# Seven-product FFN1 in two more tiles, seeded PSUM in the last two, and adding DMA stores for four output tiles

## The chip, the cores and the metric

One core of a Trainium2 chip runs the kernel. The metric is the device time of one execution in microseconds (us). Five engines take part, each with its own queue of instructions in a fixed order: PE (matrix multiply), ACT (activations and copies), DVE (elementwise), POOL (here almost only issuing DMAs) and SP (issuing DMAs). PE writes to PSUM, which ACT and DVE read.

## The reference

Attention with 16 extra "beacon" keys in front of each sequence, followed by a two-layer network with an ELU between, on 8 batches, 8 heads, 576 tokens and head size 64:

```python
k_all = np.concatenate([beacon_k, k], axis=2)          # 16 + 576 keys
v_all = np.concatenate([beacon_v, v], axis=2)
scores = scale * np.matmul(q, k_all.transpose(0, 1, 3, 2))
scores = np.where(causal, -1000000000.0, scores)
a = np.exp(scores - scores.max(-1, keepdims=True))
a /= a.sum(-1, keepdims=True) + 1e-09
attn_out = np.matmul(a, v_all)
x = attn_out.transpose(0, 2, 1, 3).reshape(4608, 512)
h = x @ w_in                                           # FFN1: 512 -> 2048
g = np.where(h > 0.0, h, np.exp(np.minimum(h, 0.0)) - 1.0)
out = g @ w_out                                        # FFN2: 2048 -> 512, fp32
```

## The kernel before

All matrix work is in fp16 or bf16 with fp32 sums in PSUM. The whole program is one list of words, written out as a string and passed to `run`; each word calls one step, and every engine executes its instructions in the order in which the list issues them. A word names a step and its arguments: `P.8.2.5` is step `P` for tile 8, group 2, phase 5. A `.v` at the end puts the step on DVE where it would otherwise be on ACT.

The 4608 tokens are cut into ten tiles: tiles 0 and 1 have 256 tokens, tiles 2 to 9 have 512. Batches of attention (steps `T`, `S`, `x`, `m`, `D`, `L`, `n`, `W`, `M`) fill the tiles' activations `xT` and run interleaved with the network of earlier tiles.

FFN1 of a tile has two forms.

- **Plain**: `F.t.i` multiplies 128 rows of `w_in` with all 512 tokens: 4 matmuls of 128x512 into one PSUM bank (`hps`). ACT takes the exponential (`e`), ACT or DVE the ReLU (`u`), and DVE joins them into the ELU (`k`). Sixteen `F` make a tile.
- **Seven products** (Strassen's scheme, in tiles 8 and 9): a group `g` covers the work of four `F` as a 2x2 block product, with 7 phases `P.t.g.0` to `P.t.g.6` of 4 matmuls of 128x256 each. The four quarters of the result are sums of products that share terms. `PF` lists for each phase the accumulator (0 or 1) and the operands. `K` takes the intermediate sums out: after phases 0, 2 and 3 a copy to SBUF on ACT (`fm`, in the buffers named `kst`/`qst` in the trace), after phases 1, 4 and 5 a DVE addition of accumulator 1 or 0 and such a copy (`hb`). `E`, `U` and `V` then do for each quarter what `e`, `u` and `k` do; they read `hb` in SBUF, or, for phase 6, PSUM. `X` (four per tile, DVE) and `H` (16, DVE) prepare the operands' differences.

FFN2 uses seven products in all tiles: `Q.t.k0.k1` issues matmuls k0 to k1 of the tile's 112, each 128x256, into two accumulators (`ops`). `Z` (DVE, four per tile) prepares differences, and `J` takes results out in the same manner as `K`: phases 0, 2, 3 are copied to SBUF (`sm`), phases 1, 4, 5 are added on DVE to such a copy (`osb`, line 635), phase 6 is copied, and `osb` is stored to `out` by SP.

PSUM has eight banks: two for `hps`, two for `ops`, and two double banks with the tag `S` for attention. Both accumulators of a group of seven products hold the two `hps` banks.

Of the kernel before, what the change touches and what calls it, by code (L numbers as in the profile page):

```python
# [17 lines left out]
def kernel(  # L18
# [11 lines left out]
    nc = tc.nc  # L30
# [487 lines left out]
    def flat(y):  # L518
        return y.rearrange("c n w -> c (n w)")
# [101 lines left out]

    @step
    def J(t, ph, eng="s"):

        if ph in (0, 2, 3):
            sm[t, ph] = melt.tile([P, 2, HM], FP32, tag="sm", name="sm")
            for q_, y in both(xy[t, PH[ph][0]]):
                (nc.scalar.copy if eng == "s" else nc.vector.tensor_copy)(out=sm[t, ph][:, q_, :], in_=y)
            return
        osb = melt.tile([P, 2, HM], FP32, tag="osb", name="osb")  # L630
        for q_, y in both(xy[t, PH[ph][0]]):
            if ph == 6:
                (nc.scalar.copy if eng == "s" else nc.vector.tensor_copy)(out=osb[:, q_, :], in_=y)
            else:
                nc.vector.tensor_tensor(  # L635
                    out=osb[:, q_, :], in0=y, in1=sm[t, {1: 0, 4: 3, 5: 2}[ph]][:, q_, :], op=ALU.add)
        i, m_ = {1: (0, 0), 4: (1, 1), 5: (0, 1), 6: (1, 0)}[ph]
        row = (tiles[t][0] if t > 1 else 0) + 256 * i
        nc.sync.dma_start(
            out=out[row:row + 256, HM * m_:HM * (m_ + 1)].rearrange("(q p) m -> p q m", p=P), in_=osb)  # L640
# [45 lines left out]
    def X_(t, n, eng="v"):  # L686
# [6 lines left out]
          (0, (1, 0), 3, False), (1, 4, (1, 1), False), (0, (1, 1), 4, False)]  # L693
    hx, fm, hb = {}, {}, {}

    @step
    def P_(t, g, ph):
        if (t, g, 0) not in hx:
            for n_ in (0, 1) if g % 2 == 0 else (1, 0):
                hx[t, g, n_] = bank("hps", name="hps").rearrange("c (n w) -> c n w", n=2)  # L700
        n_, a_, b_, first = PF[ph]
        for c in range(2):
# [9 lines left out]
    def K_(t, g, ph, eng="s"):  # L712
        src = flat(hx[t, g, PF[ph][0]])
# [8 lines left out]
    def hsrc(t, g, ph):  # L722
        return flat(hx[t, g, 0]) if ph == 6 else hb[t, g, ph]
# [76 lines left out]
    wm.4 wm.4 warm.4 wm.4 lq.0.0.0.4 lq.0.1.0.4 wm.4 warm.4 ident lq.0.0.4.8 wm.4 T.0.1.0 bt  # L800
    warm.4 lq.0.1.4.8 bk cb.0.3 T.0.0.0 cb.0.1 cb.0.0 ck.0.1.0 S.0.1.0 ck.0.0.0 T.0.1.1 x.0.1.0
    S.0.0.0 x.0.0.0 T.0.0.1 cq.0.1.1 S.0.1.2 cq.0.0.1 T.0.3.0 S.0.0.2 x.0.1.2 T.0.2.0 x.0.0.2
    cq.0.3.0 S.0.0.3 cb.0.2 lq.1.0.0.4 S.0.3.0 T.0.3.1 cq.0.2.0 x.0.0.3 lv.0.0.1 cq.0.3.1
    x.0.3.0 T.0.2.1 S.0.0.1 tri wm.4 x.0.0.1 S.0.3.2 x.0.3.2 S.0.1.3 cq.0.2.1 x.0.1.3 wm.4 wm.4
    S.0.2.0 wm.4 wm.4 x.0.2.0 S.0.3.3 wm.4 x.0.3.3 S.0.2.3 x.0.2.3 wm.4 m.0.3.0 S.0.3.1 cb.1.0
    x.0.3.1 lv.0.2 m.0.1.0 m.0.2.0 m.0.0.0 L.0.A m.0.1.2 n.0.A m.0.0.2 T.1.0.0 wi.2 m.0.3.2
    cq.1.0.0 S.0.2.1 W.0.A.1 x.0.2.1 W.0.A.0 S.0.1.1 x.0.1.1 T.1.1.0 M.0.A.1 S.0.2.2 M.0.A.0
    x.0.2.2 F.0.5 cq.1.1.0 e.0.5 lv.0.3.4 m.0.2.2 wi.1 m.0.0.3 m.0.1.3 S.1.5 S.1.1 x.1.5 m.0.3.3
    F.0.4 x.1.1 lq.1.0.4.8 wi.0 m.0.2.3 L.0.B cb.1.1 e.0.4 W.0.B.1 n.0.B S.1.3 cb.1.3 u.0.4.v
    M.0.B.1 u.0.5.v F.0.2 x.1.3 e.0.2 r.0.2 S.1.4 x.1.4 S.1.0 x.1.0 F.0.3 T.1.3.0 ck.1.3.0  # L810
    W.0.B.0 g.0.2 wi.3 k.0.4 S.1.12 m.1.0.0 k.0.5 M.0.B.0 e.0.3 F.0.1 x.1.12 T.1.2.0 S.1.10
# [133 lines left out]
```

## Time and profile before

| what | value |
|---|---|
| time, median of 3 runs | 330.33 us (329.78 to 330.42) |
| the profiled execution | 329.86 us, with a span of 328.2 us |
| instructions | 8827 |
| granted TensorE clock | 1.00 throughout |
| data moved by DMA | 34.65 MB, mean 106 GB/s |
| DMA engines' busy share | 0.9 or more in the first 18 of 40 slices, 0.0 to 0.3 in the last 16 |

The span is what the profile covers; 1.66 us of the execution lie around it. "Busy" counts overlapping instructions of an engine once. Two instructions that follow each other without a wait overlap by some tens of nanoseconds, so that the step from start to start is shorter than the mean duration that a row gives.

### The profile page before, as it was taken

Reading aid. Unit: us, or ns where it says so; the run is one execution under the profiler, and the core shown is the slowest. Engines: PE = TensorE matmul, PEld = TensorE weight load, DVE = VectorE, ACT = ScalarE, POOL = GpSimd, SP = SyncE. Lnnn points to the kernel's source line nnn. Section 1 sums busy time; section 2 is a strip of 40 time slices with the busy share of each in tenths; the row PEclk is TensorE's granted clock in tenths of the full one; section 3 lists DMA queues with packets and bytes.
Section 4 is the critical chain, followed back from the end, with each engine's and each line's share of the span. In section 5 each row is a group of like instructions: output and inputs, shape, how many; then the busy total and the mean of one; then the engine's idle time right before and its main releaser. Section 6 shows DMA issues by size and latency. Waiting matters only on the chain.

```text
span 328.2 us, 8827 instructions
## 1 busy us (share of the span) xinstructions
PE 318.5 (97%) x3648; PEld 215.7 (66%) x3648; DVE 296.9 (90%) x527; ACT 276.4 (84%) x449; POOL 85.2 (26%) x109
## 2 busy tenths in 40 slices
PE   7879999999999999999999999999999999999995
PEld 4656766566555655566555665566665888888884
DVE  2677998999998999999989989999999999999992
ACT  2979999998889897999999888988699598889930
POOL 8973791742705626004010500000000000000000
PEclk9999999999999999999999999999999999999999
DMA  9999999999999999995922792010110021111113
GB/s 115 169 190 206 172 167 185 151 151 154 174 173 154 136 172 151 188 116 61 160 82 58 77 106 84 12 34 2 66 34 33 2 96 34 34 65 34 35 64 128
DMA packets 130520, 34.65 MB, mean 106 GB/s; under 512 B 112816, under 2 KB 130480, under 8 KB 130480
## 3 DMA queue, kind: packets, MB, share of 16 engines
q0 software_dynamic: 95840, 18.49, 69.1%
q1 hardware_dynamic: 33920, 15.34, 23.8%
q8 instruction: 28, 0.46, 0.6%
q10 hardware_dynamic: 720, 0.26, 0.3%
q14 instruction: 12, 0.10, 0.1%
HBM read 37.22 MB, written 15.34 MB: 160 GB/s over the span
## 4 chain that ended last, share of the span: by engine, by line
PE 72%; DMA 12%; ACT 7%; POOL 4%; DVE 3%; issue 2%; DVEq 0%; POOLq 0%
PE ops L618 27%; PE hps L514 22%; DMA v<-in_v_dram 10%; PE hps L706 8%; PE sc L318 5%; ACT et L333 5%; PE ut L376 5%; PE sx L618 2%; POOL scr L769 1%; POOL v L149 1%; DMA kst<-in_k_dram 1%; ACT e L524 1%; POOL w_out L163 1%; DVE qkp L396 1%; PE lt L422 1%
## 5 line engine op out<-in xcount | busy, mean ns | idle before, releaser
L333 ACT ACTIVATE et<-sc 128x1024 f16<-128x1024 f32 (+2 forms) x114 | 104.2, 968 | 8.1 <-PE sc L318 7.6
L514 PE MATMUL hps<-xT,w_in 128*128 128x512 f16 (+1 forms) x512 | 110.7, 353 | 0.3 <-DVE gt L556 0.3
L618 PEld LDWEIGHTS <-gt 128*128 128x128 f16 x864 | 83.0, 98 | 21.1 <-issue 2.9
L524 ACT ACTIVATE e<-hps 128x512 f32<-128x512 f32 x112 | 66.7, 615 | 9.0 <-PE hps L514 4.1
L514 PEld LDWEIGHTS <-w_in 128*128 128x128 f16 x512 | 46.8, 98 | 39.0 <-issue 5.5
L544 DVE SCALAR_TENSOR_TENSOR gt<-e,r 128x512 f16<-128x512 f32 x103 | 68.6, 683 | 2.2 <-ACT e L524 0.7
L618 PE MATMUL ops<-w_out,gt 128*128 128x256 f16 x416 | 54.7, 273 | 0.0
L618 PE MATMUL ops<-wt,gt 128*128 128x256 f16 x400 | 53.6, 273 | 0.0
L530 ACT ACTIVATE r<-hps 128x512 f16<-128x512 f32 x74 | 45.0, 616 | 4.5 <-PE hps L514 4.3
L149 POOL DMA_DIRECT2D v<-in_v_dram x40 | 36.4, 1016 | 3.5 <-DMA v<-in_v_dram 1.9
L566 DVE TENSOR_TENSOR gt<-gt 128x2048 f16<-128x2048 f16 (+1 forms) x30 | 33.1, 1110 | 0.1
L338 DVE TENSOR_TENSOR et<-et,triu 128x1024 f16<-128x1024 f16 (+4 forms) x66 | 26.6, 447 | 1.8 <-ACT et L333 1.7
L532 DVE TENSOR_SCALAR r<-hps 128x512 f16<-128x512 f32 x29 | 19.9, 685 | 4.0 <-ACT e L524 3.2
L376 PEld LDWEIGHTS <-v 128*32 128x32 f16 (+1 forms) x800 | 17.2, 96 | 9.4 <-issue 1.2
L745 DVE SCALAR_TENSOR_TENSOR gt<-e,r 128x512 f16<-128x512 f32 x32 | 21.5, 683 | 0.5 <-ACT kst L716 0.4
L376 PE MATMUL ut<-et,v 128*32 128x464 f16 (+3 forms) x560 | 21.1, 296 | 0.3 <-DMA v<-in_v_dram 0.3
L396 DVE TENSOR_TENSOR qkp<-qkp,et 128x1344 f16<-128x1344 f16 (+2 forms) x33 | 19.2, 583 | 0.4
L635 DVE TENSOR_TENSOR osb<-ops,sm 128x512 f32<-128x512 f32 x26 | 17.7, 682 | 1.3 <-PE ops L618 1.3
L716 ACT COPY kst<-hps 128x512 f32<-128x512 f32 x24 | 13.9, 589 | 4.8 <-PE hps L706 4.6
L474 DVE TENSOR_TENSOR xT<-ut,rl 128x672 f16<-128x672 f32 (+12 forms) x26 | 16.4, 669 | 0.7 <-PE ut L376 0.4
L618 PE MATMUL ops<-w_out,s 128*128 128x256 f16 x128 | 16.9, 273 | 0.0
L618 PEld LDWEIGHTS <-s 128*128 128x128 f16 x144 | 13.9, 98 | 2.5
(118 smaller groups left out, 415.7 us busy)
## 6 DMA issues: line engine op xcount, KB each, us to landing
out_dram<-osb SPq DMA_DIRECT2D x35, 256.0 KB, 2.2
v<-in_v_dram POOLq DMA_DIRECT2D x24, 128.0 KB, 11.8
scr<-in_q_dram POOLq DMA_DIRECT2D x5, 576.0 KB, 16.2
scr<-in_k_dram POOLq DMA_DIRECT2D x5, 576.0 KB, 18.1
w_in<-in_moe_w_in_dram POOLq DMA_DIRECT2D x8, 256.0 KB, 8.7
w_out<-in_moe_w_out_dram POOLq DMA_DIRECT2D x4, 512.0 KB, 10.5
qst<-in_q_dram POOLq DMA_DIRECT2D x4, 288.0 KB, 9.6
kst<-in_k_dram POOLq DMA_DIRECT2D x4, 288.0 KB, 10.0
```

The source lines that it names most:

```text
L149: nc.gpsimd.dma_start(out=vt[b][r0:r0 + n, j, :, :], in_=v[b, :, ilo[j]:ilo[j] + n, :].rearrange("h s d -> s h d"),)
L333: nc.scalar.activation(out=ets[b, d][:, :, a - EC2 * d:e - EC2 * d], in_=sc[b, g][:, :, a - c0:e - c0], func=AFT.Exp, bias=0.0, scale=SCALE)
L338: nc.vector.tensor_tensor(out=o, in0=o, in1=i, op=ALU.mult)
L376: nc.tensor.matmul(out=t[32 * i:32 * (i + 1), a - qa:e - qa], lhsT=ones[0:kc[j], :] if half is None else v16[0:kc[j], j, h, half:D:2], rhs ...
L396: nc.vector.tensor_tensor(out=o, in0=t[0:rows, :, a:e] if n == 0 else o, in1=t[0:rows, :, col:col + e - a], op=ALU.add)
L514: nc.tensor.matmul(out=h[:, n_, :], lhsT=w_in16[:, cc, P * fc:P * (fc + 1)], rhs=xt[k][:, cc, a - TT * k:e - TT * k], start=(cc == 0), sto ...
L524: nc.scalar.activation(out=eb[t, i], in_=flat(hp[t, i]), func=AFT.Exp, bias=0.0, scale=1.0)
L530: nc.scalar.activation(out=rb[t, i], in_=flat(hp[t, i]), func=AFT.Relu, bias=0.0, scale=1.0)
L544: nc.vector.scalar_tensor_tensor(out=half(t, i), in0=eb[t, i], scalar=1.0, in1=rb[t, i], op0=ALU.subtract, op1=ALU.min)
L566: (nc.vector if eng == "v" else nc.gpsimd).tensor_tensor(out=o_, in0=a_, in1=b_, op=op_)
L618: nc.tensor.matmul(out=half_of(xy[t, n_], qd), lhsT=lw[:, P * qd:P * (qd + 1)], rhs=wt_[:, c, :], start=(first and c == 0 and (qd == 0 or ...
L706: nc.tensor.matmul(out=hx[t, g, n_][:, c, :], lhsT=lw, rhs=rh, start=(first and c == 0 and k_ == 0), stop=(k_ == 1), skip_group_check=True)
```

## The change

Three edits, and a new order of the list.

1. Seven products for 15 groups instead of 8: the first three groups of tile 6 and all four of tile 7 take this form, besides tiles 8 and 9. In tile 6 the plain form is left for `F.6.12` to `F.6.15`. For each of these groups 16 matmuls of 128x512 become 28 of 128x256.
2. In tiles 8 and 9 phase 0 gets an accumulator of its own (`sa`, in the tag `S`, which attention has left by then). `K.t.g.0` is now a ScalarE copy from `sa` to a `hps` bank, and phase 1 accumulates on it. `K.t.g.1`, the DVE addition, is gone, and `E` and `U` of phase 1 read that bank. Phases 3 and 5 take another `hps` bank.
3. In tiles 5 to 8 the partial sums are no longer added on DVE. The copy `sm` is stored to its block of `out` by SP, the second part is copied by ACT to `osb`, and POOL issues a DMA that adds it to what stands in `out`.

```diff
+    TA = (5,6,7,8)
...
     def J(t, ph, eng="s"):
...
+            if t in TA:
+                nc.sync.dma_start(out=block(t, {0: 1, 3: 4, 2: 5}[ph]), in_=sm[t, ph])
             return
         osb = melt.tile([P, 2, HM], FP32, tag="osb", name="osb")
         for q_, y in both(xy[t, PH[ph][0]]):
-            if ph == 6:
+            if ph == 6 or t in TA:
                 (nc.scalar.copy if eng == "s" else nc.vector.tensor_copy)(out=osb[:, q_, :], in_=y)
...
+        if ph == 6 or t not in TA:
+            nc.sync.dma_start(out=block(t, ph), in_=osb)
+        else:
+            nc.gpsimd.dma_start(out=block(t, ph), in_=osb, accum_op=ALU.add)
...
+    PA = [0, 1, 0, 2, 0, 2, 0]
...
     def P_(t, g, ph):
-        if (t, g, 0) not in hx:
+        seed = t >= 8
+        if seed and ph == 0:
+            hx[t, g, 0] = psum.tile([P, 2, 512], FP32, tag="S", name="sa")[:, 0, :].rearrange("c (n w) -> c n w", n=2)
+        if seed and ph == 3:
+            hx[t, g, 2] = bank("hps", name="hps").rearrange("c (n w) -> c n w", n=2)
+        if not seed and (t, g, 0) not in hx:
...
         n_, a_, b_, first = PF[ph]
+        if seed:
+            n_ = PA[ph]
+            first = first and ph != 1
...
     def K_(t, g, ph, eng="s"):
-        src = flat(hx[t, g, PF[ph][0]])
+        if t >= 8 and ph == 0:
+            hx[t, g, 1] = bank("hps", name="hps").rearrange("c (n w) -> c n w", n=2)
+            nc.scalar.copy(out=flat(hx[t, g, 1]), in_=flat(hx[t, g, 0]))
+            return
+        src = flat(hx[t, g, (PA[ph] if t >= 8 else PF[ph][0])])
...
     def hsrc(t, g, ph):
+        if t >= 8 and ph == 1:
+            return flat(hx[t, g, 1])
...
-    Q.9.49.56 J.9.2.v Z.9.4.1 Z.9.4.0 J.8.5 Q.9.63.70 J.9.3 Q.9.70.77 Q.9.77.84 Q.9.84.91 J.9.4
+    Z.9.1.1 Q.9.0.7 Q.9.7.14 Z.9.2.0 J.8.6 Q.9.14.21 J.8.5 Z.9.2.1 Q.9.21.28 J.9.0 Q.9.28.35
```

The list is new from its first words on: the attention of the first batches, which ReLUs stand on DVE, and the places of the loads differ too. What each engine executes stays the same in kind outside the three edits, apart from four FFN1 results whose ELU was taken by `r` and `g` (both on DVE) and is now taken by `u` and `k`.

ACT, in FFN1 of tile 9, before. `kst0` and `qst0` are SBUF buffers for the sums, `hps` PSUM banks, `e` and `r` the two parts of the ELU:

```order
L716 COPY kst0_88<-hps_5264 128x512
L735 ACTIVATE r_5319<-kst0_88 128x512
L728 ACTIVATE e_5321<-kst0_88 128x512
L728 ACTIVATE e_5335<-qst0_87 128x512
L735 ACTIVATE r_5341<-hps_5263 128x512
L735 ACTIVATE r_5358<-qst0_87 128x512
L728 ACTIVATE e_5360<-hps_5263 128x512
L716 COPY kst0_88<-hps_5353 128x512
```

The same engine in the last group of tile 9 now; `sa` is the accumulator of the phases 0, 2, 4 and 6:

```order
L733 COPY hps_5484<-sa_5458 128x512
L752 ACTIVATE e_5498<-qst0_87 128x512
L738 COPY kst0_88<-hps_5477 128x512
L738 COPY kst0_88<-sa_5458 128x512
L635 COPY sm_5521<-ops_5278 128x512
L759 ACTIVATE r_5525<-hps_5484 128x512
L752 ACTIVATE e_5527<-hps_5484 128x512
L759 ACTIVATE r_5529<-qst0_87 128x512
```

The first copy of a group goes from PSUM to PSUM, and one exponential and one ReLU of the group read PSUM where they read SBUF; ACT's number of instructions for such a group is the same.

DVE at the last group of tile 9 before (`gt` is the ELU's result):

```order
L719 TENSOR_TENSOR kst0_88<-hps_5353,kst0_88 128x512
L745 SCALAR_TENSOR_TENSOR gt_5172<-e_5360,r_5341 128x2x256
L719 TENSOR_TENSOR qst0_87<-hps_5352,kst0_88 128x512
L745 SCALAR_TENSOR_TENSOR gt_5172<-e_5414,r_5399 128x2x256
L745 SCALAR_TENSOR_TENSOR gt_5172<-e_5428,r_5426 128x2x256
L566 TENSOR_TENSOR gt_5172<-gt_5172 128x4x256
```

and now:

```order
L741 TENSOR_TENSOR qst0_87<-hps_5477,kst0_88 128x512
L769 SCALAR_TENSOR_TENSOR gt_5321<-e_5498,r_5482 128x2x256
L741 TENSOR_TENSOR kst0_88<-sa_5458,kst0_88 128x512
L566 TENSOR_TENSOR s3_86<-gt_5321 128x1024
L769 SCALAR_TENSOR_TENSOR gt_5321<-e_5531,r_5529 128x2x256
L769 SCALAR_TENSOR_TENSOR gt_5321<-e_5527,r_5525 128x2x256
```

Of the three additions of a group (line 719, now 741) two are left in tiles 8 and 9.

The end of POOL's queue, now; `v` is the load of a batch's values, which was the last entry before:

```order
L149 DMA v_3635<-in_v_dram 80x8x64
L649 DMA out_dram<-osb 128x2x256 x12
```

The twelve adding stores stand behind all loads, so that no load waits for them.

246 lines of the change are left out of this document (127 added, 119 removed).

## The prediction

> **What bounds the kernel now.** The first view is the busy time of each engine by stages of the span. Its columns are PE, PE's weight loads, DVE, ACT and POOL, then the granted clock, the DMA engines' share and GB/s.
>
> ```profile
> 20.00:40.00 20.00, 17.96 (x332) 12.93 (x325) 16.21 (x35) 18.11 (x25) 10.52 (x16) 1.00 1.40 193
> 40.00:60.00 20.00, 19.85 (x348) 12.77 (x346) 18.14 (x34) 19.39 (x32) 10.93 (x12) 1.00 1.69 172
> 60.00:200.00 140.00, 139.08 (x1466) 84.07 (x1465) 133.49 (x228) 127.09 (x197) 46.10 (x52) 1.00 1.44 131
> 200.00:240.00 40.00, 39.75 (x430) 24.26 (x431) 38.51 (x64) 32.65 (x55) 0.00 (x0) 1.00 0.10 34
> 240.00:300.00 60.00, 60.00 (x543) 48.65 (x544) 59.13 (x102) 51.09 (x98) 0.00 (x0) 1.00 0.13 42
> 300.00:312.00 12.00, 12.00 (x111) 10.64 (x109) 11.65 (x20) 11.71 (x23) 0.00 (x0) 1.00 0.12 38
> ```
>
> PE is never idle from 240 to 312 us and for 1.2 us in the 180 us before. DVE is close behind: 0.9 us idle of 60 in the stage where tiles 8 and 9 run seven products. A busy PE row is modelled, so the second view is the chain of work that ended last, where pieces stand from start to start.
>
> ```profile
> 250.54 0.76 PE ops L618 x7
> 251.30 1.73 PE hps L514 x8
> 253.03 0.77 PE ops L618 x7
> ...
> 281.41 1.53 PE ops L618 x14
> 282.94 0.87 PE hps L706 x8
> 283.81 0.77 PE ops L618 x7
> ...
> 322.83 1.76 PE sx L618 x16
> ```
>
> Each piece begins where the one before ends: PE is a gapless queue at 1.73/8 = 0.216 us for a 128x512 matmul (plain FFN1) and 0.87/8 = 0.109 us for a 128x256 one (seven products, and FFN2). So PE's own work is the bound, and DVE could become it with little more.
>
> **Part 1, seven more groups.** A group of plain FFN1 is 16 x 0.216 = 3.46 us on PE; by seven products it is 28 x 0.109 = 3.05. All seven are on the path: 7 x 0.41 = **-2.9 us**, if nothing makes PE wait. That a half-length matmul costs a half, weight load included, is what line 706 shows in tiles 8 and 9.
>
> What it adds elsewhere are the steps that take the products out. I price an instruction by the step from start to start without a wait, from the timeline:
>
> ```profile
> 298.17 0.59 ACT L728 ACTIVATE e<-hps 128x512 f32<-128x512 f32 x1
> ...
> 298.65 0.60 ACT L735 ACTIVATE r<-hps 128x512 f16<-128x512 f32 x1
> ...
> 298.72 1.28 DVE L745 SCALAR_TENSOR_TENSOR gt<-e,r 128x512 f16<-128x512 f32 x2
> ...
> 299.59 0.66 ACT L735 ACTIVATE r<-qst 128x512 f16<-128x512 f32 x1
> 300.12 0.65 ACT L728 ACTIVATE e<-qst 128x512 f32<-128x512 f32 x1
> ...
> 305.03 0.43 DVE L737 TENSOR_SCALAR r<-kst 128x512 f16<-128x512 f32 x1
> 305.37 0.68 DVE L745 SCALAR_TENSOR_TENSOR gt<-e,r 128x512 f16<-128x512 f32 x1
> ```
>
> ACT needs 0.48 us for 128x512 from PSUM (298.17 to 298.65) and 0.53 from SBUF; DVE 0.60 (1.28 less the 0.68 of one), but 0.34 for a ReLU from SBUF. The counts of before and the remaining durations are in the groups:
>
> ```profile
> L716 ACT COPY kst<-hps 128x512 f32<-128x512 f32 x24 | 13.9, 589 | 4.8 <-PE hps L706 4.6 <-issue 0.2
> ...
> L719 DVE TENSOR_TENSOR kst<-hps,kst 128x512 f32<-128x512 f32 x12 | 8.2, 685 | 0.5 <-PE hps L706 0.2 <-ACT kst L716 0.2
> L719 DVE TENSOR_TENSOR qst<-hps,kst 128x512 f32<-128x512 f32 x12 | 8.2, 684 | 0.2
> ...
> L635 DVE TENSOR_TENSOR osb<-ops,sm 128x512 f32<-128x512 f32 x26 | 17.7, 682 | 1.3 <-PE ops L618 1.3
> ...
> L689 DVE TENSOR_TENSOR qst<-xT 128x512 f16<-128x512 f16 x4 | 1.7, 419 | 0.0
> ...
> L551 DVE TENSOR_SCALAR r<-e 128x512 f16<-128x512 f32 x9 | 4.5, 497 | 1.5 <-ACT e L524 1.5
> ...
> L532 DVE TENSOR_SCALAR r<-hps 128x512 f16<-128x512 f32 x29 | 19.9, 685 | 4.0 <-ACT e L524 3.2 <-PE hps L514 0.3
> ...
> L149 POOL DMA_DIRECT2D v<-in_v_dram x40 | 36.4, 1016 | 3.5 <-DMA v<-in_v_dram 1.9 <-DMA w_out<-in_moe_w_out_dram 0.8 <-DMA qst<-in_q_dram 0.5
> ```
>
> The number of exponentials, ReLUs and ELU joins is that of before. New per group are three copies on ACT and three additions on DVE, and per tile four `X`.
>
> **Part 2, seeding.** It takes 8 additions from DVE (tiles 8 and 9, four groups each, phase 1); ACT's copy stays a copy. No row shows ACT writing PSUM: its nearest rows are the same read with an SBUF result, 0.59 us for the copy and 0.60 for the ReLU, and I take no difference; 8 copies that cost 0.1 more or less are 0.8 us on an engine that has idle time there. What it adds is a wait: PE's phase 1 now waits for the copy, where it needed nothing before. Queued behind it on PE are FFN2 and the other groups' phases. The order puts phases of neighbouring groups between phase 0 and phase 1, and two accumulators stand in the banks that attention has left; so I put this at nothing. Were that cover gone, each wait would be one copy, 8 x 0.59 = 4.7 us.
>
> **Part 3, adding stores.** Twelve DVE additions (four tiles, phases 1, 4, 5) become ACT copies. POOL gets 12 issues of about 1.0 us (line 149), in a time when its column above is 0.00. SP's stores stay 36 in number: 12 `osb` are replaced by 12 `sm`. Each addition waits for the landing of the store to the same block; behind it POOL has only later additions. ACT waits for a free `osb` of three; a tile uses four of them in some 25 us, so a landing of up to about 12 us is hidden. No row shows an adding DMA; the bounds are these, in KB and us to landing:
>
> ```profile
> out_dram<-osb SPq DMA_DIRECT2D x35, 256.0 KB, 2.2
> ...
> v<-in_v_dram POOLq DMA_DIRECT2D x6, 128.0 KB, 5.4
> ...
> scr<-in_k_dram POOLq DMA_DIRECT2D x5, 576.0 KB, 18.1
> ```
>
> The 18.1 us were met while the DMA engines were full; the second row is of 150 to 200 us, when they no longer were, and with a share of 0.10 to 0.13 I take 5.4. The Trainium skill, "DMA: Bandwidth & Descriptors", section "Anatomy of one DMA", gives a DMA issued from GpSimd about 2.0 us plus its bytes at 436 GB/s, an estimate of 2.6 us for 256 KB; by it too the sum gets nothing from here, and the 5.4 us row lies above it.
>
> **DVE and ACT together.** Counts of now are those of the new program. DVE: additions of `K` 24 to 37, +13 x 0.60 = 7.8; `J` -12 x 0.60 = -7.2; one copy comes and one goes; `X` 8 x 0.34 = 2.7 (0.42 less the overlap of 0.08); ReLUs from PSUM 29 to 21, -4.8, from SBUF 4 to 16, +4.1; `r` 9 to 5 at 0.42, -1.7. Sum **+0.9 us**. ACT: copies of `K` 24 to 44, +9.6; of `J` 24 to 37, +6.2; 13 exponentials more that read SBUF, +0.6. Sum **+16.4 us**.
>
> From the six stages, 20 to 312 us, DVE was idle for 292 - 277.1 = 14.9 us and ACT for 292 - 260.0 = 32.0. To end 2.9 us earlier DVE may be idle for 14.9 - 0.9 - 2.9 = 11.1 us and ACT for 32.0 - 16.4 - 2.9 = 12.7: 4% each. That is possible, since DVE ran at 1.5% idle from 240 to 300, but then ACT had 15%. Some of the saving comes back as waits of PE, between nothing (240 to 312 us show none) and all of it. In 60 to 200 us, where DVE had 4.6% and ACT 9.2%, PE waited 0.92 of 140 us; that rate over the 105 us of the new form is 0.7 us. A further 0.5 us is for this:
>
> ```profile
> 104.68 3.24 POOL L149 DMA_DIRECT2D v<-in_v_dram x3
> ...
> 105.60 1.02 DVE L551 TENSOR_SCALAR r<-e 128x512 f16<-128x512 f32 x1 [1.20 <-ACT e L524]
> ...
> 113.11 0.41 DVE L551 TENSOR_SCALAR r<-e 128x512 f16<-128x512 f32 x1
> ```
>
> The same ReLU from SBUF took 1.02 us while POOL issued DMAs, and 0.41 when it did not. The Trainium skill, "SBUF — State Buffer", section "Who interferes with whom", has this as a rule: a DVE `tensor_scalar` that uses both SBUF ports and GpSimd shut each other out for a whole instruction. It speaks against moving ReLUs to this form beside new POOL issues, and the trace agrees with 1.02 against 0.41. Here 16 such ReLUs meet 12 issues of 1.0 us in some 105 us: 16 x 12 x (1.0 + 0.4)/105 = 2.6 meetings at up to 0.6 us, 1.5 us at most, of which I take a third on the path.
>
> **Sum.** 328.2 - 2.9 + 0.7 + 0.5 = 326.5 us of span; with the 1.66 us around it 328.2. The profiled execution, 329.86, lay 0.47 below the median 330.33, so the median should be **328.6 us**. With none of the 1.2 given back it is 327.4.
>
> **Rivals.**
> *The saving is turned into waits* (330.3 us). PE's 2.9 us come back in full because DVE and ACT set the pace. For it: three engines at 96% with two or four PSUM banks between them. Against it: PE without a wait at 98.5% of DVE.
>
> *DVE becomes the bound in the late stretch* (slower). From 200 to 312 us DVE was idle for 112 - 109.3 = 2.7 us. The late tiles add there 21 additions in tiles 6 and 7 (12.6), `X` (2.7), the ReLUs from SBUF and one from PSUM (4.7), and lose 8 seeded additions (4.8), 12 of `J` (7.2) and 5 ReLUs of tiles 6 and 7 from PSUM (3.0): +5.0 us. If the reordering moves none of that ahead of 200 us, DVE ends 5.0 - 2.7 = 2.3 us later: 330.5 + 1.66 + 0.47 = 332.6 us; with its 2.7 us of idle kept, 335.3. The place is the groups of tiles 6 and 7: phase 3 restarts the accumulator that DVE's first addition still reads, and that addition waits for ACT's copy, 0.59 + 0.68 us behind whatever is queued. It decides as soon as DVE's work between tile 6's and tile 9's FFN1 exceeds PE's by more than the 2.7 us. Against it: the new order takes groups of tile 6 before tile 5's FFN2, so part of that work moves ahead.
>
> *More than the saving* (325.9 us). The new start removes waits of PE such as these two, 0.66 + 0.81 us, and nothing comes back:
>
> ```profile
> 20.86 0.35 PE L318 MATMUL sc<-qkp 64*128 64x320 bf16 x4 [0.66 <-ACT et L333]
> ...
> 22.53 0.32 PE L264 MATMUL tp<-identb,kst 96*64 96x96 bf16 x6 [0.81 <-issue]
> ```
>
> 330.33 - 2.9 - 1.5 = 325.9. Against it: ACT is busy for 18.1 and 19.4 of 20 us there, and its load is the same.
>
> *The last adding store ends late* (334.4 us). `J.8.5` stands after matmul 21 of tile 9's FFN2; 91 x 0.109 = 9.9 us of PE and the 4 us of tail follow. Copy and issue take 1.6 us, which leaves 12.3 for the landing; at 18.1 us the end is 5.8 us later. At 5.4 it is hidden.
>
> **How the numbers follow.** A measurement of this kernel can tell 0.2%, 0.66 us, from no change. Chances: forecast 0.46; more than the saving 0.12; waits for all of it 0.13, within 0.2%; DVE the bound 0.26; last store 0.03. Faster 0.46 + 0.12 = 0.58, same 0.13, slower 0.29. The forecast's own range is 327.4 to 329.6. The whole range goes from 326.0, near the full gain, to 333.5, above the DVE case at 332.6; what it leaves out is the far end of that case, the last store, and half of the largest gain.
>
> **What would show it.** Right: 28 matmuls of a group in 3.05 us in tiles 6 and 7, PE gapless after 200 us, DVE's busy time about 298 and ACT's about 292, adding stores that land within 12 us, and a span near 326.5. Wrong: PE's line for seven products waiting on DVE's additions (line 741) or ACT's copies (lines 733, 738) for more than 2 us in sum; ACT waiting for an `osb`; the last event a DMA of `J.8.5`; or a start, up to 60 us, that alone differs by more than 1 us.

## The result and the profile after

The changed kernel takes **326.55 us** (median of 20 executions, 325.87 to 330.37), the one before 330.58 (20 executions on the same chip): a ratio of 0.9878, with a 95% interval of 0.9854 to 0.9902. The forecast was 328.6: faster, but by 1.7 us instead of 4.0. One thing is needed to read the medians and ratios: in 43 of 112 executions of the program before and in 3 of 20 of the changed one the mean granted clock of PE was under 0.997 (0.979 to 0.995) and the span mostly 1 to 4 us longer, and the ratios leave out executions over 1.5% above the fastest of their kernel (four of the twelve of w3 below). Among executions at full clock the spans are **328.4 to 328.7 us before (five sets of runs) and 324.8 now**, 3.6 to 3.9 us apart. What is left of the 4.0 goes with that difference in clock. Below, "full-clock span" is the median span of the executions with a clock of at least 0.997.

The profiled execution of the changed kernel has a span of 324.6 us, 3.6 less than before. The first view is the page's row of busy times, before and now:

```profile
PE 318.5 (97%) x3648; PEld 215.7 (66%) x3648; DVE 296.9 (90%) x527; ACT 276.4 (84%) x449; POOL 85.2 (26%) x109
```

```profile
PE 316.2 (97%) x3731; PEld 224.7 (69%) x3732; DVE 296.0 (91%) x536; ACT 290.6 (90%) x482; POOL 101.8 (31%) x121
```

PE is busy for 2.3 us less, and idle for 1.3 us less (8.4 instead of 9.7). The forecast had PE idle for *longer*. DVE's busy time stood at 298 in the forecast and ACT's at 292: they are 296.0 and 290.6. The stages now, with the columns of the prediction's first view:

```profile
20.00:40.00 20.00, 19.04 (x370) 13.66 (x369) 15.42 (x36) 18.14 (x26) 11.56 (x16) 1.00 1.41 191
40.00:60.00 20.00, 19.22 (x332) 12.53 (x330) 18.39 (x34) 19.04 (x30) 15.15 (x15) 1.00 1.81 180
60.00:200.00 140.00, 139.85 (x1483) 83.79 (x1478) 133.66 (x228) 133.82 (x214) 43.74 (x49) 1.00 1.44 129
200.00:240.00 40.00, 40.00 (x448) 32.69 (x446) 39.58 (x73) 38.89 (x71) 3.58 (x3) 1.00 0.32 73
240.00:300.00 60.00, 60.00 (x627) 52.03 (x625) 59.60 (x104) 56.60 (x109) 8.27 (x7) 1.00 0.35 68
300.00:312.00 12.00, 12.00 (x113) 10.72 (x111) 11.83 (x20) 10.41 (x21) 2.36 (x2) 1.00 0.37 85
```

From 200 to 312 us DVE is idle for 1.0 us of 112, where it was 2.7, and PE does not wait at all. From 60 to 200 us PE's idle time fell from 0.92 to 0.15 us. Cut finer, that stretch was this before,

```profile
60.00:100.00 40.00, 39.61 (x425) 24.00 (x424) 38.49 (x63) 35.77 (x55) 18.09 (x19) 1.00 2.07 158
100.00:165.00 65.00, 64.47 (x685) 38.61 (x684) 62.61 (x109) 60.03 (x94) 22.37 (x26) 1.00 1.50 141
```

and is this now:

```profile
60.00:100.00 40.00, 40.00 (x424) 24.31 (x419) 36.35 (x58) 38.59 (x62) 18.67 (x20) 1.00 2.01 156
100.00:165.00 65.00, 65.00 (x711) 39.04 (x709) 63.50 (x112) 61.94 (x98) 20.36 (x24) 1.00 1.48 137
```

The chain of work that ended last shows the late stretch as a gapless queue, now with seven products in pieces of four and eight; its last piece of matmuls, which was at 322.83, is now at 319.25:

```profile
284.84 0.87 PE sa L724 x8
285.71 0.87 PE hps L724 x8
286.59 0.56 PE sa L724 x4
287.14 1.53 PE ops L618 x14
288.67 0.87 PE sa L724 x8
...
319.25 1.76 PE sx L618 x16
```

The costs of the new operations, from the groups (busy time, mean ns of one, idle time ahead) and the DMA issues:

```profile
L738 ACT COPY kst<-hps 128x512 f32<-128x512 f32 x28 | 17.1, 616 | 1.5 <-issue 0.5 <-PE hps L724 0.4 <-DVE kst L741 0.4
L733 ACT COPY hps<-sa 128x512 f32<-128x512 f32 x8 | 4.6, 578 | 0.3 <-PE sa L724 0.3
L761 DVE TENSOR_SCALAR r<-kst 128x512 f16<-128x512 f32 x9 | 3.8, 421 | 0.1
L649 POOL DMA_DIRECT2D out_dram<-osb x12 | 14.2, 1185 | 113.5 <-ACT osb L642 92.1 <-ACT r L759 9.8 <-ACT hps L733 9.3
...
out_dram<-osb SPq DMA_DIRECT2D x23, 256.0 KB, 3.1
out_dram<-sm SPq DMA_DIRECT2D x12, 256.0 KB, 2.2
out_dram<-osb POOLq DMA_DIRECT2D x12, 256.0 KB, 4.3
```

The seeding copy (line 733) is a little shorter than the copy to SBUF, an adding store is issued in 1.19 us and lands in 4.3.

### The profile page after: what moved, and what is told of

Its sections match the earlier page's. It is cut to its first block, busy times and chain, and to the rows that moved or that the text cites. A ratio compares the mean times of both kernels' runs of the same rounds, so it can differ in the third digit from the quotient of the medians.

```text
span 324.6 us, 9075 instructions
## 1 busy us (share of the span) xinstructions
PE 316.2 (97%) x3731; PEld 224.7 (69%) x3732; DVE 296.0 (91%) x536; ACT 290.6 (90%) x482; POOL 101.8 (31%) x121
## 4 chain that ended last, share of the span: by engine, by line
PE 87%; ACT 5%; DVE 4%; DMA 1%; issue 1%; POOL 1%; DVEq 0%; POOLq 0%
PE ops L618 32%; PE hps L514 20%; PE hps L724 10%; PE sc L318 8%; PE ut L376 6%; PE sa L724 4%; ACT et L333 4%; PE sx L618 2%; PE lt L376 2%; DMA kst<-in_k_dram 1%; DVE et L338 1%; PE lt L422 1%; ACT e L524 1%; DVE r L532 1%; DVE gt L544 1%
## 5 line engine op out<-in xcount | busy, mean ns | idle before, releaser
L333 ACT ACTIVATE et<-sc 128x1024 f16<-128x1024 f32 (+2 forms) x114 | 105.5, 980 | 4.1 <-PE sc L318 3.7
L514 PE MATMUL hps<-xT,w_in 128*128 128x512 f16 (+1 forms) x400 | 83.9, 346 | 0.2
L514 PEld LDWEIGHTS <-w_in 128*128 128x128 f16 x400 | 36.4, 98 | 27.2 <-issue 3.6
L544 DVE SCALAR_TENSOR_TENSOR gt<-e,r 128x512 f16<-128x512 f32 x79 | 52.6, 683 | 2.0 <-ACT r L530 1.1
L524 ACT ACTIVATE e<-hps 128x512 f32<-128x512 f32 x84 | 50.1, 620 | 2.8 <-PE hps L514 1.7
L649 POOL DMA_DIRECT2D out_dram<-osb x12 | 14.2, 1185 | 113.5 <-ACT osb L642 92.1
L149 POOL DMA_DIRECT2D v<-in_v_dram x40 | 35.7, 943 | 16.6 <-DMA scr<-in_q_dram 5.1
L769 DVE SCALAR_TENSOR_TENSOR gt<-e,r 128x512 f16<-128x512 f32 x60 | 39.5, 681 | 0.0
L530 ACT ACTIVATE r<-hps 128x512 f16<-128x512 f32 x59 | 35.9, 622 | 2.1 <-PE hps L514 1.9
L338 DVE TENSOR_TENSOR et<-et,triu 128x1024 f16<-128x1024 f16 (+5 forms) x66 | 27.1, 447 | 1.9 <-ACT et L333 1.9
L724 PEld LDWEIGHTS <-w_in 128*128 128x128 f16 x240 | 23.1, 98 | 3.8 <-issue 0.2
L738 ACT COPY kst<-hps 128x512 f32<-128x512 f32 x28 | 17.1, 616 | 1.5 <-issue 0.5
L474 DVE TENSOR_TENSOR xT<-ut,rl 128x672 f16<-128x672 f32 (+12 forms) x26 | 16.4, 668 | 1.3 <-PE ut L376 1.2
```

The lines of the kernel that those rows point to most:

```text
L149: nc.gpsimd.dma_start(out=vt[b][r0:r0 + n, j, :, :], in_=v[b, :, ilo[j]:ilo[j] + n, :].rearrange("h s d -> s h d"),)
L333: nc.scalar.activation(out=ets[b, d][:, :, a - EC2 * d:e - EC2 * d], in_=sc[b, g][:, :, a - c0:e - c0], func=AFT.Exp, bias=0.0, scale=SCALE)
L338: nc.vector.tensor_tensor(out=o, in0=o, in1=i, op=ALU.mult)
L514: nc.tensor.matmul(out=h[:, n_, :], lhsT=w_in16[:, cc, P * fc:P * (fc + 1)], rhs=xt[k][:, cc, a - TT * k:e - TT * k], start=(cc == 0), sto ...
L524: nc.scalar.activation(out=eb[t, i], in_=flat(hp[t, i]), func=AFT.Exp, bias=0.0, scale=1.0)
L530: nc.scalar.activation(out=rb[t, i], in_=flat(hp[t, i]), func=AFT.Relu, bias=0.0, scale=1.0)
```

## The experiments

The theory: PE alone is the bound; the saving stays because edits 2 and 3 keep DVE just under it, and the new order has taken early waits of PE away. The rivals: DVE has room and needs no such relief; or the late form alone makes the whole gain. In each expectation A is the theory for that run, and the other letters are its rivals, as the text tells them. All results in one table; "loss" is the full-clock span less that of the program it was made from (324.8, or before's in the same set of runs). The 324.8 us are of one set, and before's own span moved by 0.3 us between the sets, so a loss on the changed kernel is known to some 0.3 us.

| run | median us | ratio to before, 95% interval | full-clock span (executions) | loss |
|---|---|---|---|---|
| changed kernel | 326.55 | 0.9878, 0.9854 to 0.9902 | 324.8 (17 of 20) | |
| x1_noadd | 333.24 | 1.0072, 1.0044 to 1.0100 | 331.5 (6 of 6) | +6.7 |
| x2_dveadd | 333.94 | 1.0116, 1.0075 to 1.0157 | 331.95 (4 of 6) | +7.1 |
| z4_edit1_alone | 338.86 | 1.0230, 1.0196 to 1.0264 | 337.15 (6 of 6) | +12.3 |
| w1_add_three_tiles | 328.23 | 0.9945, 0.9911 to 0.9978 | 326.35 (8 of 12) | +1.5 |
| w2_add_two_tiles | 330.36 | 0.9982, 0.9952 to 1.0011 | 328.0 (9 of 12) | +3.2 |
| z3_add_five_tiles | 327.98 | 0.9919, 0.9883 to 0.9956 | 326.0 (7 of 9) | +1.2 |
| y4_before_add | 332.51 | 1.0027, 0.9994 to 1.0061 | 329.3 (5 of 12) | +0.9 on before |
| x3_plain4 | 332.37 | 1.0052, 1.0026 to 1.0077 | 330.55 (10 of 12) | +5.7 |
| x4_plain7 | 337.55 | 1.0238, 1.0191 to 1.0285 | 335.8 (4 of 6) | +11.0 |
| w3_after_v_late | 331.99 | 1.0005, 0.9966 to 1.0045 | 327.25 (2 of 12) | +2.4 |
| y3_before_v_early | 331.78 | 1.0013, 0.9979 to 1.0048 | 329.0 (7 of 12) | +0.6 on before |
| w4_before_relu_form | 330.69 | 0.9998, 0.9970 to 1.0027 | 328.9 (9 of 12) | +0.4 on before |
| y1_early_new | 331.99 | 1.0033, 1.0003 to 1.0064 | 329.4 (7 of 12) | +1.0 on before |
| y2_early_old | 338.23 | 1.0198, 1.0154 to 1.0243 | 336.0 (4 of 6) | +11.2 |
| z1_first_old_102 | 335.87 | 1.0137, 1.0095 to 1.0178 | 332.0 (1 of 6) | +7.2 |
| z2_first_new_102 | 336.42 | 1.0162, 1.0113 to 1.0211 | none of 6 | |
| v1_before_fillers | 331.02 | 1.0006, 0.9990 to 1.0023 | 329.3 (12 of 12) | +0.65 on before |
| v2_after_fillers | 326.86 | 0.9874, 0.9851 to 0.9898 | 325.2 (5 of 5) | +0.4 |

### DVE's load: edits 2 and 3 taken back

x1, w1 and w2 undo edit 3 in all four tiles, in tile 5, and in tiles 5 and 6; z3 extends it to tile 4; y4 puts it into the program before.

```diff
-    TA = (5,6,7,8)
+    TA = ()            # x1;  w1: (6,7,8)  w2: (7,8)  z3: (4,5,6,7,8)
```

> The changed kernel with the adding stores undone: in tiles 5 to 8 the partial sums are added on DVE again (12 additions, +7.2 us of DVE; 12 copies less, -5.6 us of ACT), all else and the order as changed. Theory A (PE's work is the bound and DVE only just keeps up: 1.0 us idle of 112 from 200 to 312 us): DVE becomes the bound, +4 to +6 us on the changed kernel's 326.5, so 330.5 to 332.5. Theory B (PE's work alone counts, DVE has room): 326.5 to 327.0.

> The changed program with adding stores in tiles 6 to 8 only: tile 5's three additions are on DVE again (+1.8 us), its three copies off ACT (-1.4 us), between 205 and 233 us. Theory H (DVE's load is at its limit: all but the 1.0 us that it is idle comes out): 326.5 + 0.8 = 327.3 us. Rival K (threshold: no loss until some more is put on): 326.5 us. Rival L (ACT is what was tight there, as with adding stores in tile 4): 326 us.

> The changed program with adding stores in tiles 7 and 8 only: six additions on DVE again (+3.6 us), six copies off ACT. Theory H: 326.5 + 3.6 - 1.0 = 329.1 us. Rival K (threshold): 326.5 to 327.5 us. Taking all twelve back had cost 6.7 us.

Additions of 1.8, 3.6 and 7.2 us put back on DVE cost 1.5, 3.2 and 6.7 us: all of it but 0.3 to 0.5 us, from the first step on, and more than theory H's 0.8 and 2.6. There is no threshold; w1's copies taken off ACT brought nothing. From 200 to 312 us DVE is busy for 111.0 of 112 us in the changed kernel and for 111.1 to 111.2 in w1, w2 and x1: it was full already, and what is added there comes behind. With edit 3 undone the stage of 240 to 300 us reads

```profile
240.00:300.00 60.00, 57.73 (x596) 48.88 (x594) 59.66 (x104) 51.25 (x96) 0.00 (x0) 1.00 0.11 37
```

DVE is as full as in the changed kernel (59.60), but PE is idle for 2.3 us, while ACT has 8.7 us to spare. So DVE at 99% was no sign of PE waiting, and neither of room: the changed kernel stands within half a microsecond of DVE as the bound.

x2 undoes edit 2: the accumulators stay, but the copy goes to SBUF and DVE adds again. z4 undoes 2 and 3 together, so that edit 1 stands alone.

```diff
-            nc.scalar.copy(out=flat(hx[t, g, 1]), in_=flat(hx[t, g, 0]))
+            nc.scalar.copy(out=sb3[g % 2], in_=flat(hx[t, g, 0]))
             return
+        if t >= 8 and ph == 1:
+            nc.vector.tensor_tensor(out=sb3[2], in0=flat(hx[t, g, 1]), in1=sb3[g % 2], op=ALU.add)
+            return
```

> The changed kernel with the seeding undone in tiles 8 and 9, its three accumulators and its order kept: phase 0 is copied to SBUF, phase 1 has a bank of its own, and DVE adds the two (8 additions, +4.8 us of DVE, none on ACT or PE; PE's wait for the copy goes). Theory A: +3 to +4.5 us, 329.5 to 331.0. Theory B: 326.5. If the wait of phase 1 for the copy had cost something, it would come out below 326.5.

> The changed program with edits 2 and 3 both taken back, so that the seven products in tiles 6 and 7 stand alone: DVE has 8 additions of the last two tiles (4.8 us) and 12 of the outputs (7.2 us) again, ACT twelve copies less; words in the new order, three accumulators kept. Theory H (DVE's load is the bound, of which 1.0 us was idle from 200 to 312 us): 326.5 + 12.0 - 1.0 = 337.5 us. Rival I (the chain copy, addition, ReLU adds its own waits, as when edit 2 alone was taken back): 326.5 + 6.7 + 7.4 = 340.6 us. Rival J (one relief would do, so the two losses do not add): 334 us.

x2 loses more than its 4.8 us of additions, 7.1. PE's waits by what they waited for (us in total, times, longest), and the longest of ACT's, from 200 us on:

```profile
PE sa L727 <- ACT kst L743: 1.5, 2, 1.1
PE hps L727 <- DVE kst L738: 1.1, 2, 0.8
PE hps L727 <- ACT kst L743: 0.9, 1, 0.9
...
ACT r L764 <- DVE kst L738: 3.7, 4, 1.2
```

PE waits 2.4 us for later copies on ACT and 1.1 us for the additions themselves (line 738), and ACT's ReLUs wait 3.7 us for these additions. So the chain copy, addition, ReLU is longer, and holds ACT; that the copies queued behind the ReLUs come late by it is argued from ACT's fixed order, as is that another list would avoid it. Together (z4) the loss is 12.3 us for 12.0 us of DVE work: between H's 11.0 and I's 14.1, a little nearer to H, and less than the 13.8 of the two losses as measured. Edit 1 alone, in this order, is thus 2.3% slower than the kernel before: the rival "DVE becomes the bound" is what happens to it without the other two edits. A list written for edit 1 alone was not run.

> The changed program with adding stores in tile 4 too: three additions of 0.60 us less on DVE (1.8 us) and three copies of 0.47 us more on ACT, at 165 to 205 us. Theory A (PE is the bound): 326.5 us, no difference over 0.2%. Rival D (DVE's 99% holds PE a little): 325.5 us. Rival E (ACT or the storing queue pays): 327 us or more.

> The program before with the adding stores of tiles 5 to 8 alone (edit 3, order as before, seven products in tiles 8 and 9 only). It takes 7.2 us from DVE where PE did not wait. Theory A (PE bound by itself from 200 us on): 330.2 us, no difference over 0.2%. Rival D (DVE's load held PE in before too): 2 us less, 328.4. Rival E (twelve more copies on ACT, or the adding stores' issues on POOL beside ReLUs, cost): 331 or more.

The relief of DVE is worth something only where DVE is the limit. One tile more (z3) costs 1.2 us, and 200 to 220 us, where two of its three copies stand, shows a part of it:

```profile
200.00:220.00 20.00, 19.50 (x249) 14.88 (x244) 17.90 (x36) 19.45 (x35) 3.58 (x3) 1.00 0.29 54
```

Now DVE has room (2.1 us) and ACT has not (0.55), and PE waits for 0.5 us, 0.3 of it for such a copy. In the program before (y4), where DVE did not hold PE, edit 3 costs 0.9 us. Rival E is right in both; whether ACT's copies or POOL's issues cost it in y4 was not separated.

### The seven products taken back

x3 writes tile 7's four groups in the plain form, x4 all seven of tiles 6 and 7, each word at the place of the phase that it replaces. Part of `w_in` holds differences by then, which the plain groups there multiply, so these two kernels do not compute the reference's result; the work is the same.

```diff
-    Q.5.70.77 X.7.3 P.7.0.1 P.7.0.0 J.5.3 Q.5.77.84 X.7.2 V.6.2.1
+    Q.5.70.77 F.7.0 J.5.3 Q.5.77.84 V.6.2.1
```

> The changed kernel with the four groups of tile 7 in the plain form again, words in the same places: PE +4 x 0.41 = +1.7 us, DVE -8.5, ACT -5.8. If PE's work is the bound before and after, 328.2. If the trace's mean pitch holds, in which a plain matmul that follows other work starts 0.1 us late (0.465 us a group), 328.4. If DVE or ACT had been taking back a part of the saving, less than 1.2 us more, under 327.7.

> The changed kernel with all seven added groups (tiles 6 and 7) in the plain form again, seeding, adding stores and order kept: PE does the work of the kernel before. Theory A with an early part (the new order of the first 165 us removes about 1 us of PE's waits): 326.5 + 2.9 = 329.4, which leaves 1.1 us to the kernel before. If the whole gain is the groups': 330.6. If the mean pitch of 0.465 us a group holds: 329.8.

Both lost far more than the saving: 5.7 and 11.0 us. The stage of 240 to 300 us of x3:

```profile
240.00:300.00 60.00, 56.84 (x554) 44.82 (x552) 51.06 (x85) 48.74 (x93) 7.08 (x6) 1.00 0.31 58
```

PE is idle for 3.2 us while DVE has 8.9 and ACT 11.3 us to spare. Its longest waits from 200 us on are these:

```profile
PE hps L514 <- ACT r L530: 1.9, 2, 1.2
PE sa L724 <- ACT hps L733: 1.1, 1, 1.1
```

No engine is the bound; the list no longer fits what it orders, as far as such waits show it. These two runs do not measure what a group saves, and I had expected them to.

### The early waits and the order

Two words of the load of batch 2's values changed places between the kernels. w3 puts the load back in the changed kernel, y3 puts it forward in the kernel before.

```diff
 # w3
-    x.2.5 k.2.13 u.2.7 lv.2.0.1 u.2.5
+    x.2.5 k.2.13 u.2.7 u.2.5
...
-    x.2.7 wt.3.1 lv.3.2.3.4 F.2.10
+    x.2.7 wt.3.1 lv.3.2.3.4 lv.2.0.1 F.2.10
 # y3
-    M.1.0.0 u.1.2 W.1.1 lv.2.2.3.4 u.1.4
+    M.1.0.0 u.1.2 W.1.1 lv.2.0.1 lv.2.2.3.4 u.1.4
```

> The changed program with one word moved: the second part of batch 2's values is loaded where it was before. Theory A (PE waits 0.9 us for it at 82 us again): 327.4 us. Rival B (the wait is taken up behind it, as in the reverse move, which brought nothing): 326.5 us.

> The program before with one word moved: the second part of batch 2's values is loaded right ahead of that batch's last key load, as in the changed program. PE's waits of 0.30 + 0.62 us at 82 us were for this load. Theory A: they go and nothing takes them back, 329.5 us. Rival C (another load is late instead, since the DMA engines are full up to 150 us, or the next wait takes it): 330.4 us.

In w3 the wait is back, longer than in the kernel before, and PE is idle for 1.5 us in a stage where it was gapless:

```profile
83.27 0.28 PE L376 MATMUL lt<-et,v 128*32 128x112 f16 x8 [1.29 <-DMA v<-in_v_dram]
...
84.00 0.85 PE L376 MATMUL ut<-et,v 128*32 128x464 f16 x20 [0.25 <-DMA v<-in_v_dram]
```

The profiled span is 326.7 us, 2.1 more than that of the changed kernel, and no later wait takes it up: w3 is 0.3 us behind the changed kernel at the start of FFN2 of tile 1 (60 us), 2.2 us at that of tile 2 (98 us), and stays 2.2 us behind at every later tile. With PE gapless behind it, an early wait reaches the end in full. That is more than theory A's 0.9. In y3 the reverse move brought nothing. In its profile another wait has come in the load's place, and the clock fell behind it (rows of 3 us; the clock is the column of 0.97 and 0.50):

```profile
86.84 0.38 PE L618 MATMUL ops<-wt,gt 128*128 128x256 f16 x2 [1.98 <-DVE wt L566]
```

```profile
84.50:87.50 3.00, 1.02 (x10) 0.38 (x7) 3.00 (x6) 0.77 (x2) 2.33 (x4) 0.97 2.38 152
87.50:90.50 3.00, 3.00 (x15) 0.99 (x14) 2.54 (x7) 2.01 (x4) 2.60 (x5) 0.50 2.40 166
```

So the load's place is worth something only together with the order around it (rival C). In w3's median of 331.99 there is more than the wait: 10 of its 12 executions were under a clock of 0.997.

w4 tests the other early suspect, the results that DVE took in two steps behind each other:

```diff
-    S.3.5 x.3.5 m.3.0.0 r.3.2 Q.2.28.35 F.3.8 g.3.2 F.3.12
+    S.3.5 x.3.5 m.3.0.0 u.3.2.v Q.2.28.35 F.3.8 k.3.2 F.3.12
```

> The program before, with the eight FFN1 results of tiles 0 to 5 that it takes by two dependent steps on DVE and the changed program doesn't taken by ReLU and join, in the same places; DVE's work rises by 8 x 0.18 = 1.4 us. Theory A (these steps hold PE's banks, and their waits at 104 to 114 us go): 329.6 us. Rival M (DVE's additional work comes out, or the ReLU stands in the way where the minimum stood): 331.5 us. Rival B (neither reaches the end): 330.4 us.

No gain (+0.4 us at full clock): rival B. These are eight of before's nine such results; the changed kernel has five such results, four of them others. Alone and in the old order this suspect is out.

Four runs mix the two orders. y1 and z2 are the program before with the first 728 or 458 words of the new list, and the words that are left in the old order; y2 and z1 are the changed program with the first 731 or 461 words of the old list.

```diff
-    <the old list>
+    <words 1 to 728 of the new list> <what is left of the old list, in its order>
```

> The program before, with the new order alone up to the end of FFN2 of tile 3 (about 160 us; ReLUs and loads placed as now), then the words that are left in the old order; none of the three edits. Theory A (some of the gain is early waits of PE that the new order does without: by the starts of tile 4's FFN2, 167.8 against 165.8 us, and PE's work up to there, 1.3 us): 329.1 us. Rival B (the whole gain comes from the seven products and what they no longer pay): 330.4 us, as before.

> The reverse: the changed program with its three edits, but the old order up to the end of FFN2 of tile 3, then the words that are left in the new order. Theory A (1.3 us of the gain is early waits): 327.8 us, and PE's waits at 82 and 104 to 114 us are back. Rival B (all of it is from the late form): 326.5 us. If the seam between the orders costs something, both this and the reverse case come out above their theory by the same kind of wait around 165 us.

> The changed program, but with the old order of the words up to about 102 us (the middle of FFN2 of tile 2), then what is left in the new order. By PE's work up to that place the new order is 1.1 us behind there (102.3 us reached in both, with 89.0 us of PE's work done before and 87.9 now). Theory A (PE alone is the bound behind it, and the new order saves its early waits between 102 and 165 us): 1.1 us less, 325.4 us. Rival B (the start does not reach the end, DVE or the DMA queues set the pace in 60 to 165 us): 326.5 us. Rival F (the seam makes PE wait for the ReLUs and loads that stand late): 328 us or more.

> The program before, with the new order of the words up to about 102 us and the old one behind it; none of the three edits. Theory A: the new order's start is 1.1 us behind and its gain lies behind 102 us, so 331.5 us. Rival G (the gain of the new order lies ahead of 102 us, where it has no wait for the values' load at 82 us): 329.5 us. Rival B: 330.4 us.

The seams cost more than what was to be measured: 2 us of PE's waits in y1, 5 to 8 in the others, all right behind the cut. Only what lies ahead of a seam can be read. In y1, with none of the three edits, the stretch of 60 to 130 us has no wait of PE, where the old order had 0.92 us; the seam then takes 2.1 us:

```profile
60.00:130.00 70.00, 70.00 (x760) 42.17 (x760) 65.69 (x108) 67.31 (x106) 27.17 (x27) 1.00 1.93 160
130.00:200.00 70.00, 67.89 (x706) 41.57 (x704) 62.72 (x108) 62.27 (x100) 15.44 (x21) 1.00 0.94 99
```

That the early waits go with the order and not with the edits is shown by this; what that is worth in the end is not, by the mixed orders.

The profiles of the other runs show it by stretches without a seam. The first instruction of the changed kernel that belongs to one of the three edits (an `X` of tile 6, on DVE) starts at 183.0 us. From the first weight load of FFN2 of tile 1 to that of tile 4 (about 60 to 166 us) it takes 105.7 us, and so do the nine other runs with the new order up to there (x1 to x4, z3, z4, w1, w2, v2: 105.7 to 105.8). With the old order it takes 108.0 us (before), 107.7 (v1) and 108.5 (w4, y4); w3, with the one load moved, takes 107.6. From there to the last matmul it is 154.9 us with the edits (the changed kernel, w3, v2, and z1 too, whose start is in the old order) and 156.3 to 156.5 us without them (before, v1, w4, y3, and z2, whose start is in the new order). So the order ahead of the edits is worth 2.0 to 2.8 us in the middle, and the edits with the order around them some 1.5 us behind.

### The granted clock

The kernel before waits for 0.66 + 0.81 us at 20 to 23 us. The new order has four filler matmuls (`warm.4`) there. v1 puts fillers at that place of the program before, v2 at 8 to 11 us of the changed one.

```diff
 # v1
-    x.0.2.1 W.0.A.0 S.0.1.1 x.0.1.1 T.1.1.0
+    x.0.2.1 W.0.A.0 wm.4 wm.4 S.0.1.1 x.0.1.1 wm.4 wm.4 T.1.1.0
 # v2
-    S.0.0.0 T.0.0.1 ... S.0.0.2 ... S.0.1.2 ... S.0.1.3
+    S.0.0.0 wm.4 T.0.0.1 ... wm.4 S.0.0.2 ... wm.4 S.0.1.2 ... wm.4 S.0.1.3
```

> The program before with sixteen more filler matmuls (128x128, their result is not used, 0.9 us of PE) at 20 to 22 us, where PE waits 0.66 + 0.81 us and where other runs showed the clock at 0.50 for 3 us behind such a wait. Theory N (too little work there makes the clock fall in some executions, and the new order's fillers prevent it): the share of executions with a clock under 0.997 falls from 4 in 10 to 1 in 10 or less, the span at full clock stays 328.4 us, and the median falls by 0.3 to 0.5 us. Rival O (the fall has nothing to do with that wait): the share stays 4 in 10 and the median 330.4, or 0.5 us more for the fillers.

> The changed program with sixteen more filler matmuls (0.9 us of PE) at 8 to 11 us, where PE waits 0.26 to 0.30 us at a time and the clock fell to 0.50 for 7 to 13 us in other runs with this start. Theory N: no execution with a clock of 0.979 to 0.989 any more (about 2 in 10 now), the median stays at 326.5 us. Rival O: 2 in 10 stay, or the fillers delay the start by up to 0.9 us: 327.4 us.

With the fillers none of 12 executions of v1 was under 0.997, against 7 of 17 of the program before on the same chip: that fillers at this place prevent the fall is shown, as theory N has it. But the fillers cost 0.65 us at full clock, so the median stayed. v2 had none in 5 where 3 in 20 were expected, which tells nothing, and costs some 0.4 us. Neither beats the changed kernel, and no other run does.

## Why the prediction was right or wrong

**The saving on PE** (7 x 0.41 = 2.9 us) is borne out by the steps of the trace; no run measures it by itself, since x3 and x4 lost far more. PE's work, summed by steps without a wait as in the prediction, is 303.9 us before and 301.0 now: that confirms the counts, since the prices are the same. The mean steps behind 120 us, 0.2233 us for a plain matmul and 0.111 for one of the seven products, would make 16 x 0.2233 - 28 x 0.111 = 0.46 us of a group and 3.2 of seven; what this is more than 0.41 is small gaps that the other count holds as waits.

**The step that failed is what is given back: +1.2 us in the forecast, -0.6 measured.** From the start of FFN2's first weight load in tiles 1 and 4 and of the last matmul, less PE's work up to each place (priced in the same way, so good to some tenths):

| stretch | before: time, work | now: time, work | PE's waits |
|---|---|---|---|
| to FFN2 of tile 1 | 59.8, 47.7 | 60.1, 47.1 | +0.9 |
| from there to FFN2 of tile 4 | 108.0, 102.2 | 105.7, 102.2 | -2.2 |
| from there to the last matmul | 156.5, 154.0 | 154.9, 151.7 | +0.7 |

The late stretch gave back 0.7 where 1.2 stood. The larger part of the miss, 1.3 us, is what the sum put at nothing: the order ahead of 165 us. I had taken the rate of waits from 60 to 200 us and put it on the new form, which was the wrong pattern: those waits belonged to places in the old order, not to DVE's load of 95%. The prediction treated everything ahead of 165 us as unchanged but for the rival "more than the saving"; that rival (325.9 us, a chance of 0.12) came nearest to 326.55. Its mechanism was half right and its place wrong, so its number was in part luck: early waits did go, but those at 82 and 100 to 165 us, while the start that it named is 0.9 us worse, and 0.7 us did come back. Of the 2.2 us the views show 0.92 as idle time of PE; the rest are gaps that the modelled busy time covers. How they divide stays open: w3 shows that the load's place alone is worth 2 us in the new order, y3 that it is worth nothing in the old one.

**The meetings of ReLUs with POOL's issues** (0.5 us) were nearly nothing. Three ReLUs from SBUF overlapped an issue, and one was slow:

```profile
286.22 0.58 DVE L761 TENSOR_SCALAR r<-qst 128x512 f16<-128x512 f32 x1
```

It took 0.58 us, against 0.42 in the mean: 0.16 us in all. The kernel before had a second such case too, which the prediction did not use: a ReLU at 155.6 us, beside POOL's issues, took 0.52 us, not 1.02. So 0.6 us a meeting was the worst case, not the common one. The rule of the Trainium skill that the prediction cites ("SBUF — State Buffer", section "Who interferes with whom") would have a ReLU that starts during an issue wait for it; two of the three did start so (the third began 0.06 us before its issue), and the trace agrees for one of them, not for a whole instruction.

**DVE and ACT.** DVE's sum was forecast at +0.9 us and is -0.9 in busy time, ACT's at +16.4 and is +14.2. That DVE could carry the late stretch at 99% was argued from 240 to 300 us of the profile, and holds. That it would then be within 0.5 us of the limit (w1, w2) was not seen; the forecast had counted on 11 us of idle time.

**Seeding** was rightly put at nothing: no wait of PE for line 733 stands in the trace, and the copy takes 578 ns, not 589. **Adding stores**: 1.19 us an issue instead of 1.0, and a landing of 4.3 instead of 5.4 us, both hidden; the last is issued at 310.24 us and the span ends 14 us later. The estimate of 2.6 us from the Trainium skill, "DMA: Bandwidth & Descriptors", section "Anatomy of one DMA", was short by 1.7; the plain stores of the same size took 2.2 and 3.1 us here.

**The rivals on the slow side** fell, and x1, x2 and z4 show what held them off: with the additions on DVE the kernel would have been at 333 to 339 us, where the prediction had 332.6 to 335.3 for DVE as the bound.

## What to carry to other kernels

Where several engines stand at 97 to 99%, busy shares tell neither who waits nor how much room is left; a dose of work put back in steps does, and here all but half a microsecond of it came out. When a change brings a new order of everything, compare PE's waits stretch by stretch from the first on: with a gapless queue behind it, an early wait reaches the end in full. An order written for one set of operations loses more when an operation is swapped in place (x3: 5.7 us, with no engine full) than the operation itself is worth.

## What the runs showed of the hardware

The granted clock fell to 0.50 behind stretches in which PE was far from idle. The rows of y4, a fall, and of the program before, none (same places; PE's busy time stands first, the clock behind POOL's):

```profile
20.00:23.40 3.40, 1.69 (x66) 1.27 (x58) 1.87 (x3) 2.02 (x3) 2.77 (x5) 0.98 1.60 192
23.40:26.70 3.30, 3.30 (x25) 1.65 (x24) 3.19 (x12) 1.78 (x3) 1.40 (x3) 0.50 1.30 202
```

```profile
20.00:23.40 3.40, 1.92 (x47) 1.34 (x40) 2.03 (x4) 1.90 (x4) 2.34 (x4) 1.00 1.61 191
23.40:27.00 3.60, 3.41 (x69) 2.38 (x70) 2.59 (x12) 3.49 (x5) 1.83 (x3) 1.00 1.30 205
```

PE busy for 1.69 of 3.4 us lost the clock for the next 3.3 us, and 1.92 kept it. But so did less, in w4 at the same place:

```profile
20.00:23.40 3.40, 1.40 (x40) 0.94 (x32) 1.51 (x4) 1.51 (x2) 2.35 (x4) 1.00 1.57 194
```

So the amount of work in such a stretch does not decide it. The Trainium skill, "TensorE: Matmul & The Clock Gate", "Part 1: The HAM clock gate (the "warmup" mystery)", has the clock fall after an idle window of about 3.4 us; the length of the fall agrees with that window here, the condition does not, since PE was busy for half of it. z2 had a single wait of 2.7 us without a fall (PE busy for 0.72 us from 103.0 to 106.4 us, the clock 1.00 behind it), so the wait's length alone does not decide; what does is not settled.

By rows of 1 us the falls of y3, y4 and z2 last 3.4 us each, those at the start of w1 and x4 6.8 and 13.6 us, two and four times as long. A fall of 3.4 us to half the clock takes about 0.005 off the mean of a span of 328 us (estimated from these rows), and the mean clocks under 0.997 lie mostly near 0.995, 0.990, 0.985 and 0.979. A mean clock of 0.994 or 0.995 goes mostly with 1 to 2 us of time.

A copy on ACT from PSUM to PSUM (578 ns) is no slower than one to SBUF (616 ns in the same kernel).
